# Cosine and sine parts in the two partition halves: three transform stages of a spectral block as pairs of half-array matmuls

## The chip, the cores and the metric

The kernel runs on one core of a Trainium2 chip. The metric is the device time of one execution in microseconds (us), as the median of several runs. TensorE is called PE here, its weight loads PEld; VectorE is DVE, ScalarE ACT, GpSimd POOL, and SyncE SP, whose instructions are almost all DMA issues.

## What is computed

The reference is one block, forward and backward. Its forward half takes x (2048 tokens of 512 channels), normalises the rows and modulates them, filters them in the frequency domain, and sends the sum through a second normalisation and a two-layer network with a squared ReLU. All gradients are returned too.

```python
def _A_ref(x, w_r, w_i):                     # spectral filter
    X = rfft2(x.astype(float32), axes=(-2, -1))      # 2048 x 257, complex
    X = X * (w_r + 1j * w_i)
    return irfft2(X, s=(2048, 512)).astype(bfloat16)
def _B_ref(x, w1, b1, w2, b2):               # 512 -> 1792 -> 512
    h = relu(x @ w1 + b1) ** 2
    return h @ w2 + b2
h = layernorm(x) * (1 + ca) + sa;  x = x + ga * _A_ref(h, w_r, w_i)
h = layernorm(x) * (1 + cb) + sb;  out = x + gb * _B_ref(h, w1, b1, w2, b2)
# returned: out, and the gradients of x, w_r, w_i, w1, b1, w2, b2, c, w_mod
```

The gradient of the filter is a transform of the same kind, so transforms run twice: a forward pass and a backward pass.

## The kernel before

The Fourier transforms are done as matmuls with tables of cosines and sines. A token's number is split as p*16 + t, with p on the 128 partitions and t counting 16 tiles. The forward transform has three stages:

- f1 (`spec_f1_half`, L289, in the forward pass; `spec_f1_row`, L281, in the backward pass): 128-point transform over p. The result goes to UT, with 128 channels on the partitions.
- f2 (L324 to L338): transform over the channels with the table Cd. For each of 8 groups gi and two halves hh, four matmuls (L332) take a 128x128 block of UT as weights and stream 128 columns of Cd; the cosine columns go to the first 256 columns of a PSUM bank, the sine columns to the rest. ACT then copies both banks (L336) to AE with a factor, once per group. One matmul more (L329) adds the constant term in the first group of the forward pass.
- f3 (`f3`, L311 to L323): the 16 tiles are combined with the twiddle table LF. For each gi, hh and each of the two output parts o (real, imaginary), two matmuls of 257 columns (L318) add the cosine and the sine part up in PSUM; this takes LF in three variants, the third being the negated first, which ACT makes (L248, L1175, L1318). ACT copies the result out (L320), and DVE multiplies it with the filter (`cmul`, L411 to L418).

The inverse has g1 (`spec_g1`, L342), g2 (L367, matmuls in L372) and g3 (L378, L382). In g1, for each of 16 n = 2*gi+hh, four matmuls of 128 columns (L352) and two of 256 (L355) take 128x128 blocks of the filtered spectrum Z as weights and stream the table LG, again in three variants (L855, L1354). DVE and ACT copy its PSUM tiles to CS in turn (L360, L362).

The rest of PE's time goes to the two-layer network: L841 (products with the output's gradient, "back products", which fill gaps in the first transform), L1013 and L1042 (the two layers and their gradients), L1287 and L1386 (weight gradients, which fill gaps in the second transform). Column sums (L908, L1238, L1396, L1444) use a quarter of the array's columns each, four at a time, by `tile_position=(0, q)` with q = 0, 32, 64, 96; L459 uses one row strip.

The order of the work is not left to the program text. `ORDER` (L477) lists, for each of PE, ACT, DVE, POOL and SP, the numbers of its instructions as the program emits them, in the order in which they are to run; `set_order` (L574) chains them. Each engine works through its list strictly in that order. Data dependencies are kept with semaphores beside it. The lists hold 2428 matmuls, 470 ACT, 775 DVE and 52 POOL instructions and 290 DMA issues of SP.

Two forms of the code matter for the change, the inner loops of f3 and of g1:

```python
for cs in range(2):                                                              # L317
    nc.tensor.matmul(ps[:, o, 0:DF], lhsT=K["LF"][gi][:, o + cs, hh, :],
                     rhs=ae[:, hh, 256 * cs:256 * cs + DF], start=(cs == 0), stop=(cs == 1))
for ri in range(2):                                                              # L351
    nc.tensor.matmul(ps[:, 0, P * y:P * y + P], lhsT=Z[gi][:, hh, ri, 2 * y:255 + 2 * y:2],
                     rhs=K["LG"][:, n // 4, ri + y, n % 4, :], start=(ri == 0), stop=(ri == 1))
```

Of the kernel before, what the change touches and what calls it, by code (L numbers as in the profile page):

```python
# [9 lines left out]
AF = mybir.ActivationFunctionType  # L10
# [32 lines left out]
def w_parts(rows, gi):  # L43

    v = rows.rearrange("(q h g) f -> q h g f", h=2, g=16)
    if gi > 0:
        return [(0, 64, v[:, :, gi, :]), (64, 64, v[:, ::-1, 16 - gi, :])]
    c = rows.rearrange("(q c g) f -> q c g f", c=4, g=16)
    return [(0, 64, v[:, :, 0, :]), (64, 32, c[:, 0:2, 8, :]), (96, 32, c[:, 3:1:-1, 8, :])]
# [25 lines left out]
def build_basic(tc, constp):  # L75
# [10 lines left out]
    nc.vector.memset(K["ones_q"][:, 0:1], 1.0)  # L86
    pid = constp.tile([P, 1], I32, name="pid")
# [8 lines left out]
def build_ta(tc, K, constp, g, pspool):  # L96
    nc = tc.nc
    kh = g.tile([P, 8, 2, 2, 4], I32, name="kh")
    for r in range(2):
        nc.gpsimd.iota(kh[:, :, :, r, :], pattern=[[1, 8], [16, 2], [32, 4]], base=0, channel_multiplier=0)  # L100
    for h, (base, step) in enumerate(((8, 48), (24, 16))):
        nc.gpsimd.iota(kh[:, 0, h, :, 2:4], pattern=[[0, 2], [step, 2]], base=base, channel_multiplier=0)
    nc.gpsimd.iota(kh[:, 0, 0, 1, 0:1], pattern=[[0, 1]], base=64, channel_multiplier=0)
    off = g.tile([P, 8, 2, 2, 4], I32, name="kh_off")
    nc.gpsimd.memset(off[:, :, :, 0, :], 96)
    nc.gpsimd.memset(off[:, :, :, 1, :], 0)
    nc.gpsimd.memset(off[:, 0, 0, 1, 0:1], 96)
    v = g.tile([P, P], I32, name="ta_v")
    nc.vector.scalar_tensor_tensor(out=v, in0=kh.rearrange("p a h r b -> p (a h r b)"), scalar=K["pidf"],
                                   in1=off.rearrange("p a h r b -> p (a h r b)"), op0=ALU.mult, op1=ALU.add)  # L110
# [13 lines left out]
def build_cd(tc, K, cpool, g):  # L124
# [3 lines left out]
    nc.gpsimd.iota(fr[:, 0:256], pattern=[[2, 2], [2, 128]], base=0, channel_multiplier=0)  # L128
# [13 lines left out]
    nc.vector.tensor_scalar(sn[:, 0:256:255], sn[:, 0:256:255], math.sqrt(0.5), None, op0=ALU.mult)  # L142
# [34 lines left out]
def iotas_lf(tc, g):  # L177
    nc = tc.nc
    sm = g.tile([P, 6, 4], I32, name="lf_sm")
    nc.gpsimd.iota(sm[:, 0, :], pattern=[[1, 4]], base=0, channel_multiplier=0)  # L180
    nc.gpsimd.iota(sm[:, 1, :], pattern=[[-1, 4]], base=3, channel_multiplier=0)
    nc.gpsimd.iota(sm[:, 2, :], pattern=[[0, 2], [1, 2]], base=0, channel_multiplier=0)
    nc.gpsimd.iota(sm[:, 3, 0:2], pattern=[[1, 2]], base=0, channel_multiplier=0)
    nc.gpsimd.iota(sm[:, 3, 2:4], pattern=[[-1, 2]], base=1, channel_multiplier=0)
    nc.gpsimd.iota(sm[:, 4, 0:2], pattern=[[1, 2]], base=2, channel_multiplier=0)
    nc.gpsimd.iota(sm[:, 4, 2:4], pattern=[[-1, 2]], base=3, channel_multiplier=0)
    krs = []
    for q in range(4):
        kr = g.tile([P, 2, 2, 2, 64], I16, name="lf_kr", bufs=4)
        nc.gpsimd.iota(kr[:, :, :, 0, :], pattern=[[1, 2], [16, 2], [32, 64]], base=2 * q, channel_multiplier=0)  # L190
        nc.gpsimd.iota(kr[:, :, :, 1, :], pattern=[[-1, 2], [-16, 2], [32, 64]], base=32 - 2 * q, channel_multiplier=0)
        if q == 0:
            nc.gpsimd.iota(kr[:, 0, :, 1, 0:32], pattern=[[16, 2], [64, 32]], base=8, channel_multiplier=0)
# [5 lines left out]
def build_lf(tc, K, cpool, g, sm, krs):  # L199
    nc = tc.nc  # L200
    V = nc.vector
    ti = g.tile([P, 3], I32, name="lf_ti")
    V.tensor_single_scalar(ti[:, 0:1], K["pid"], 3, op=ALU.logical_shift_right)
    V.tensor_single_scalar(ti[:, 1:2], K["pid"], 4, op=ALU.bitwise_and)
    V.tensor_single_scalar(ti[:, 2:3], K["pid"], 3, op=ALU.bitwise_and)
    tf = g.tile([P, 3], FP32, name="lf_tf")
    V.tensor_copy(tf, ti)
    t, r4, sl = tf[:, 0:1], tf[:, 1:2], tf[:, 2:3]
# [90 lines left out]
def make_ae(nc, pool):  # L299
    AEs = [pool.tile([P, 2, 514], BF16, name=f"AE{i}") for i in range(2)]  # L300
    for ae in AEs:
        nc.gpsimd.memset(ae[:, :, 256:257], 0.0)
# [1259 lines left out]
```

## Time and profile before

| what | value |
|---|---|
| time, median of 3 runs | 407.01 us (406.58 to 407.49) |
| span of the profiled execution, first to last instruction | 402.6 us |
| what lies around the span, by that median | 4.4 us |
| ACT busy | 278.5 us (69%) |
| DVE busy | 342.4 us (85%) |
| HBM traffic over the span | 36.35 MB read, 33.19 MB written |

The profile is of one execution. Busy time counts an instruction from start to end; PE's matmuls overlap (the end of one is modelled), so the distance between the starts of two matmuls tells what one costs, and the busy share does not. A row of the timeline gives the start, the length, the engine, the line, the operation, the tile written and those read, and how many like instructions were merged into it; idle time before it and what ended that stand in brackets. A row of the windows gives busy time and number of instructions for each engine in a stretch, then the granted TensorE clock, the DMA share and GB/s.

### The profile page before, as it was taken

To read this page: it belongs to the slowest core of one execution; us is meant where nothing else is said; L and a number is where in the kernel's file an instruction comes from. 1 tells how busy PE (TensorE), PEld (TensorE's weight loads), DVE (VectorE), ACT (ScalarE), POOL (GpSimd) and SP (SyncE) were. 2 spreads that over 40 slices of the span, in tenths; PEclk is the share of its full clock that TensorE was granted. 3 is DMA by queue.
4 is the path that set the end of the run, shared out by engine and by line. 5 is a ranking of instruction groups with operands and counts; after the bars stand their busy time and mean duration, and the time that the engine had idled before them with its cause. 6 is when DMAs were issued, how large, how long until landed. Compare 5 with 4: busy or idle time off the path is not lost. (4 is left out here: it accounts for less than half of the span.)

```text
span 402.6 us, 6952 instructions
## 1 busy us (share of the span) xinstructions
PE 386.3 (96%) x2428; PEld 201.8 (50%) x2428; DVE 342.4 (85%) x831; ACT 278.5 (69%) x501; POOL 14.0 (3%) x56
## 2 busy tenths in 40 slices
PE   4899999999999999999999999999999999999895
PEld 1354566665444444444444445455655675444344
DVE  5989879969897799989898999947889958897993
ACT  4559899879870596169636857457668456988693
POOL 4520100000000000000000000000000000000000
PEclk9699999999999999999999999999999999999999
DMA  8999999588595689788977889969999899999997
GB/s 255 251 208 271 232 191 270 169 192 276 140 235 140 179 230 147 216 186 210 223 193 163 192 215 239 281 170 281 315 278 283 236 326 180 182 275 234 237 278 257
DMA packets 141643, 90.97 MB, mean 226 GB/s; under 512 B 95778, under 2 KB 127528, under 8 KB 141096
## 3 DMA queue, kind: packets, MB, share of 16 engines
q1 hardware_dynamic: 140900, 89.93, 90.6%
q10 hardware_dynamic: 708, 0.59, 0.5%
q8 instruction: 19, 0.31, 0.3%
q14 instruction: 16, 0.13, 0.1%
HBM read 36.35 MB, written 33.19 MB: 173 GB/s over the span
## 5 line engine op out<-in xcount | busy, mean ns | idle before, releaser
L1287 PEld LDWEIGHTS <-h_sb 128*128 128x128 bf16 x256 | 24.7, 98 | 21.4 <-issue 0.4
L1042 PEld LDWEIGHTS <-gab 128*128 128x128 bf16 x224 | 21.5, 98 | 25.0 <-DVE gab L1020 0.6
L1013 PEld LDWEIGHTS <-w 128*128 128x128 bf16 x224 | 21.3, 98 | 25.0 <-issue 1.8
L841 PEld LDWEIGHTS <-w2T 128*128 128x128 bf16 x224 | 21.3, 98 | 22.5 <-issue 2.9
L1287 PE MATMUL mm_0s<-gab,h_sb 128*128 128x384 bf16 (+1 forms) x160 | 30.2, 342 | 0.0
L1042 PE MATMUL og_0s<-w1T,gab 128*128 128x512 bf16 x112 | 25.9, 379 | 0.1
L1042 PE MATMUL og_1s<-w1T,gab 128*128 128x512 bf16 x112 | 25.8, 379 | 0.0
L336 ACT ACTIVATE AE<-psB 128x1024 bf16<-128x1024 f32 x16 | 22.1, 1383 | 2.8 <-PE psB L332 2.8
L1013 PE MATMUL mm_1s<-h2T,w 128*128 128x512 bf16 x84 | 21.6, 379 | 0.0
L1287 PE MATMUL mm_1s<-gab,h_sb 128*128 128x512 bf16 (+1 forms) x96 | 20.8, 370 | 0.0
L1013 PE MATMUL mm_0s<-h2T,w 128*128 128x512 bf16 x80 | 20.5, 379 | 0.0
L841 PE MATMUL mm_1s<-gT_0s,w2T 128*128 128x512 bf16 x56 | 15.4, 394 | 1.1 <-DMA w2T<-in_B_w_dram 0.9
L841 PE MATMUL mm_0s<-gT_0s,w2T 128*128 128x512 bf16 x56 | 15.3, 397 | 0.8 <-DMA w2T<-in_B_w_dram 0.6
L1013 PE MATMUL pst<-h2T,w 128*128 128x512 bf16 x60 | 15.4, 379 | 0.0
L372 PEld LDWEIGHTS <-utcs 128*128 128x128 bf16 x128 | 10.3, 97 | 8.7 <-issue 2.4
L1386 PE MATMUL mm_0s<-g_sb,hn_1s 128*128 128x512 bf16 x64 | 14.5, 379 | 0.0
L841 PE MATMUL mm_1s<-gT_1s,w2T 128*128 128x512 bf16 x56 | 14.4, 379 | 0.0
L841 PE MATMUL mm_0s<-gT_1s,w2T 128*128 128x512 bf16 x56 | 14.4, 379 | 0.0
L845 ACT CAST gab<-mm_1s 128x512 bf16<-128x512 f32 x20 | 12.4, 620 | 2.2 <-PE mm_1s L841 2.2
L1386 PE MATMUL mm_1s<-g_sb,hn_0s 128*128 128x512 bf16 (+1 forms) x64 | 12.8, 352 | 0.3 <-ACT gw_0s L1387 0.3
L332 PEld LDWEIGHTS <-utcs 128*128 128x128 bf16 x128 | 9.3, 97 | 4.8 <-issue 1.8
L1386 PEld LDWEIGHTS <-hn_0s 128*128 128x128 bf16 x80 | 7.7, 98 | 6.6 <-issue 1.0
(652 smaller groups left out, 1050.2 us busy)
## 6 DMA issues: line engine op xcount, KB each, us to landing
w<-in_B_w_dram SPq DMA_DIRECT2D x2, 1792.0 KB, 8.8
Z<-wz_dram SPq DMA_DIRECT2D x4, 514.0 KB, 4.4
Xb<-xs_dram SPq DMA_DIRECT2D x4, 514.0 KB, 5.9
x_sb<-in_A_x_dram SPq DMA_DIRECT2D x2, 1024.0 KB, 6.3
n_dram<-x_sb SPq DMA_DIRECT2D x4, 512.0 KB, 5.1
h_dram<-h2r SPq DMA_DIRECT2D x8, 256.0 KB, 2.7
h_sb<-h_dram SPq DMA_DIRECT2D x4, 512.0 KB
g_sb<-in_grad_out_dram SPq DMA_DIRECT2D x2, 1024.0 KB
```

Source lines behind the costliest of these rows:

```text
L332: nc.tensor.matmul(ps[:, hh, P * co:P * co + P], lhsT=UT[:, c, 2 * gi + hh, :, :], rhs=K["Cd"][:, P * c:P * c + P], start=not extra, stop= ...
L336: nc.scalar.activation(dst, ps.rearrange("p r (s e f) -> p (r s) e f", s=2, e=2), AF.Copy, scale=EF_S)
L372: nc.tensor.matmul(ps[:, P * i:P * i + P], lhsT=CS[:, t, i].rearrange("p a b -> p (a b)"), rhs=K["Cf"][:, i, :], start=True, stop=True)
L841: nc.tensor.matmul(ps, lhsT=w2T[:, dc, fc * P:(fc + 1) * P], rhs=gT[b][:, :, dc, :], start=(dc == 0), stop=(dc == 3))
L845: nc.scalar.copy(out=gaT[b][:, fc, :], in_=ps)
L1013: nc.tensor.matmul(ps, lhsT=w1[:, dc, (fc + i) * P:(fc + i + 1) * P], rhs=h2T[b][:, :, dc, :], start=(dc == 0), stop=(dc == 3))
L1042: nc.tensor.matmul(ps, lhsT=lhs(fc), rhs=rhs[:, fc, :], start=(fc == 0), stop=(fc == NFC - 1))
L1287: nc.tensor.matmul(blocks(ps, fb), lhsT=h2_sb[:, t, dc * P:(dc + 1) * P], rhs=gh_rows(t, fb), start=(t == 0), stop=(t == NT - 1))
L1386: nc.tensor.matmul(ps[:, 0:w], lhsT=hns[fc][:, t, :], rhs=g_sb[:, t, c:c + w], start=(t == 0), stop=(t == NT - 1))
```

## The change

The cosine part of f2 now goes to the partitions 0 to 63 and the sine part to 64 to 127. UT is laid out in 32 blocks of 64 columns in place of 16 of 128. `tile_position=(0, 64 * cs)` places a matmul in one half of the array's columns, `(64 * b, 0)` in one half of its rows.

- f2: each 128-wide matmul becomes two with 64 weight columns, one for each half of the PSUM partitions: 256 matmuls of 128 columns in both passes together in place of 128.
- f3: the sum over cosine and sine part is now made inside one matmul (its 128 rows hold both), so each (gi, hh, o) has two matmuls of 64 weight columns and 257 streamed columns, one for each half of the output, in place of two full ones. LF has two variants, no negated one.
- g1: each n has 12 matmuls of 64 rows, in pairs on the two row halves: 4 of 128 columns and 8 of 64. The PSUM tile has two banks and three buffers (before: one bank, six buffers). LG has two variants.
- A POOL instruction after each copy to AE moves one column and clears another (the sine column 256). Tables that the transforms need (TA, Cd, LF) are generated in another order of rows, with more and smaller POOL instructions.
- The 12 negating copies of ACT and 4 of DVE are gone. The filter's rows are read and written in smaller pieces.
- `ORDER` is new for all five engines: 2749 matmuls, 458 ACT, 774 DVE and 84 POOL instructions and 310 DMA issues.

```diff
 def f3(gi):
     for o in range(2):
-        for cs in range(2):
-            nc.tensor.matmul(ps[:, o, 0:DF], lhsT=K["LF"][gi][:, o + cs, hh, :], rhs=ae[:, hh, 256 * cs:256 * cs + DF],
-                             start=(cs == 0), stop=(cs == 1))
+        for b in range(2):
+            m = slice(64 * b, 64 * b + 64)
+            nc.tensor.matmul(ps[m, o, 0:DF], lhsT=K["LF"][gi][:, o, hh, m], rhs=ae[:, hh, b, :], start=True, stop=True, tile_position=(0, 64 * b))
...
-            ps = psB_pool.tile([P, 2, 512], FP32, name="psB")
+            ps = psB_pool.tile([P, 2, 2, 256], FP32, name="psB")
...
-                for c in range(4):
-                    co = (0, 3, 1, 2)[c]
-                    nc.tensor.matmul(ps[:, hh, P * co:P * co + P], lhsT=UT[:, c, 2 * gi + hh, :, :], rhs=K["Cd"][:, P * c:P * c + P],
-                                     start=not extra, stop=(c == 3 if extra else True))
+                for b in (1, 0):
...
+                    for e in range(2):
+                        for cs in range(2):
+                            c = 2 * e + cs
+                            nc.tensor.matmul(ps[64 * cs:64 * cs + 64, hh, b, P * e:P * e + P], lhsT=UT[:, c, 2 * (2 * gi + hh) + b, :, :],
+                                             rhs=K["Cd"][:, P * c:P * c + P], start=not extra, stop=(e == 1 if extra else True), tile_position=(0, 64 * cs))
...
+            end = ae.rearrange("p r b f -> p (r b) f")[64:P]
+            nc.gpsimd.tensor_tensor(end[:, :, 256::-256], end[:, :, 0:1].broadcast_to([64, 4, 2]), K["one0"][64:P, None, :].broadcast_to([64, 4, 2]), op=ALU.mult)
...
 def spec_g1(tc, K, Z, CS, after=None):
-    with Slots(tc, name="psG", bufs=6, space=PSUM) as psG_pool:
+    with Slots(tc, name="psG", bufs=3, space=PSUM) as psG_pool:
...
+                def part(b, o, y, w, f0):
+                    m = slice(64 * b, 64 * b + 64)
                     for ri in range(2):
+                        yield (ps[:, b, hh, o, 64 * y:64 * y + w], Z[gi][m, hh, ri, f0:f0 + 255:2], K["LG"][m, n // 4, ri, n % 4, 64 * y:64 * y + w],
+                               ri == 0, ri == 1, (64 * b, 0))
+                for args in ((1, 0, P, 1), (0, 0, 64, 0), (0, 1, 64, 2)):
+                    for pair in zip(part(0, *args), part(1, *args)):
+                        for o, l, r, first, last, pos in pair:
+                            nc.tensor.matmul(o, lhsT=l, rhs=r, start=first, stop=last, tile_position=pos)
...
-        nc.scalar.activation(LF[:, q, 2], LF[:, q, 0], AF.Copy, scale=-1.0)
...
-        nc.vector.tensor_scalar(K["LG"][:, q, 2], K["LG"][:, q, 0], -1.0, None, op0=ALU.mult)
...
-    UT = utcs.tile([P, 4, 16, NT, 8], BF16, name="utcs")
+    UT = utcs.tile([P, 4, 32, NT, 4], BF16, name="utcs")
...
-    CS = utcs.tile([P, NT, 4, 16, 8], BF16, name="utcs")
+    CS = utcs.tile([P, 4, NT, 16, 8], BF16, name="utcs")
```

More of the change, by code (lines that the diff above doesn't have):

```diff
@@ L829 @@
     for q in range(4):
[L830 removed]
+        nc.sync.dma_start(LF_dram[q], K["LFall"][:, q])
     psM.release()
@@ L1210 @@
     gmp = Slots(tc, name="gmp", bufs=1, side="right")
-    LF2 = [lf2.tile([P, 3, 4, P], BF16, name=f"LFb{4 + 2 * g}") for g in range(2)]
+    LF2 = [lf2.tile([P, 2, 4, P], BF16, name=f"LFb{4 + 2 * g}") for g in range(2)]
     K["LF"] += [LF2[g // 2][:, :, 2 * (g % 2):2 * (g % 2) + 2] for g in range(4)]
@@ L1400 @@
         load_hn()
-    CS = utcs.tile([P, NT, 4, 16, 8], BF16, name="utcs")
+    CS = utcs.tile([P, 4, NT, 16, 8], BF16, name="utcs")
     def scale_g(gi):
```

189 lines of the change are left out of this document (98 added, 91 removed), and 156 rows, old and new, of the table ORDER.

## The prediction

> **What bounds the kernel now.** I read the page first, then the windows of the stages that the change touches, then PE's waits, then the timeline row by row for the distance between matmuls. From the page:
>
> ```profile
> span 402.6 us, 6952 instructions
> ...
> PE 386.3 (96%) x2428; PEld 201.8 (50%) x2428; DVE 342.4 (85%) x831; ACT 278.5 (69%) x501; POOL 14.0 (3%) x56
> ...
> PE   4899999999999999999999999999999999999895
> ```
>
> PE is busy from end to end; but its records overlap, so this alone proves little. The windows show the four stages that change: first f2 and f3 (50 to 74), first g1 (74 to 84), second f2 and f3 (263 to 314), second g1 (314 to 328).
>
> ```profile
> 50.00:74.00 24.00, 23.55 (x191) 15.30 (x191) 20.64 (x55) 24.00 (x37) 0.00 (x0) 1.00 0.99 205
> 74.00:84.00 10.00, 10.00 (x110) 7.96 (x109) 9.03 (x18) 7.80 (x15) 0.00 (x0) 1.00 0.80 230
> 263.00:314.00 51.00, 50.80 (x383) 29.42 (x376) 40.08 (x91) 34.77 (x56) 0.00 (x0) 1.00 0.91 265
> 314.00:328.00 14.00, 14.00 (x135) 10.32 (x134) 12.34 (x26) 7.36 (x16) 0.00 (x0) 1.00 0.97 283
> ```
>
> The columns are PE, PEld, DVE, ACT, POOL, clock. The clock is 1.00 throughout. In the first stretch ACT is busy 24.00 of 24.00 us as well, and DVE 20.64; in the others PE stands alone. PE's waits are few. The longest, and the one that a changed stage has:
>
> ```profile
> PE sm_ps L718 <- POOL ident masks.py:199: 4.0, 1, 4.0
> ...
> PE psB L332 <- ACT AE L336: 0.2, 1, 0.2
> ```
>
> So what PE need not stream comes off the end, unless ACT or DVE then ends last. What a matmul costs is the distance of starts:
>
> ```profile
> 59.12 0.61 PE L332 MATMUL psB<-Cd,utcs 128*128 128x128 bf16 x8
> 59.56 0.61 PE L318 MATMUL psC_1s<-AE,LF 128*128 128x257 bf16 x4
> 60.03 0.38 PE L318 MATMUL psC_0s<-AE,LF 128*128 128x257 bf16 x2
> 60.25 1.02 PE L841 MATMUL mm_1s<-gT_0s,w2T 128*128 128x512 bf16 x4
> ...
> 62.16 1.02 PE L841 MATMUL mm_0s<-gT_0s,w2T 128*128 128x512 bf16 x4
> 63.02 0.39 PE L318 MATMUL psC_1s<-AE,LF 128*128 128x257 bf16 x2
> ...
> 80.40 0.28 PE L352 MATMUL psG_1s<-LG,Z 128*128 128x128 bf16 x2
> 80.51 0.38 PE L355 MATMUL psG_1s<-LG,Z 128*128 128x256 bf16 x2
> 80.73 0.38 PE L355 MATMUL psG_2s<-LG,Z 128*128 128x256 bf16 x2
> ```
>
> Eight f2 matmuls take 59.56 - 59.12 = 0.44 us, 55 ns each; two f3 matmuls 60.25 - 60.03 = 0.22, 110 ns; four back products 63.02 - 62.16 = 0.86, 215 ns; in g1 128 columns 0.11 / 2 = 55 ns and 256 columns 0.22 / 2 = 110 ns. Each has its weight load, and hides it. The counts, from the groups by line (each load has one matmul):
>
> ```profile
> L332 PEld LDWEIGHTS <-utcs 128*128 128x128 bf16 x128 | 9.3, 97 | 4.8 <-issue 1.8 <-ACT utcs L286 0.4
> ...
> L352 PEld LDWEIGHTS <-Z 128*128 128x128 bf16 x128 | 9.1, 98 | 1.4 <-issue 0.2
> ...
> L318 PEld LDWEIGHTS <-LF 128*128 128x128 bf16 x64 | 5.8, 97 | 2.3 <-issue 0.3
> ...
> L318 PEld LDWEIGHTS <-LFb 128*128 128x128 bf16 x64 | 5.4, 97 | 1.7 <-issue 0.5
> ...
> L355 PEld LDWEIGHTS <-Z 128*128 128x128 bf16 x64 | 5.3, 98 | 0.4
> ```
>
> Now f2 is 128 x 55 ns = 7.0 us, f3 128 x 110 ns = 14.1 us, g1 128 x 55 + 64 x 110 ns = 14.1 us, both passes together.
>
> **The change, part by part.** Whether two half-array matmuls run side by side is the first question. The column sums already use quarters of the array's columns:
>
> ```profile
> 151.57 1.02 PE L1013 MATMUL pst<-h2T,w 128*128 128x512 bf16 x4
> 152.52 0.39 PE L908 MATMUL acc<-gp_0s,ones_q 128*32 128x512 bf16 x1
> ...
> 152.53 0.39 PE L908 MATMUL acc<-q_0s,ones_q 128*32 128x512 bf16 x1
> 152.75 0.38 PE L908 MATMUL acc<-gp_0s,ones_q 128*32 128x512 bf16 x1
> ...
> 153.19 0.38 PE L908 MATMUL acc<-q_1s,ones_q 128*32 128x512 bf16 x1
> 153.50 0.61 PE L1013 MATMUL mm_1s<-h2T,w 128*128 128x512 bf16 x2
> ```
>
> Four start within 0.01 us, the next four 0.23 us after the first: four 512-column matmuls in the time of one. Column parts do run side by side.
>
> *f3*: 128 full matmuls become 64 pairs, at 110 ns a pair 7.0 us: a gain of **7.0**.
>
> *f2*: 128 full matmuls become 128 pairs of the same width. Side by side they cost the same, and they cannot cost less, since each half streams 128 columns; one behind the other they cost 7.0 more. Taken: **0**, by the quarters.
>
> *g1*: each of 32 blocks (16 n, two passes) now has two pairs of 128 columns (55 ns each) and four of 64. For the short ones the bounds are half of 55, 28 ns, and this row:
>
> ```profile
> 10.13 0.54 PE L752 MATMUL sm_ps<-sacol,wm_2s 128*128 128x1 bf16 x16 [1.43 <-DVE sacol L722]
> 10.53 1.60 PE L737 MATMUL mod_ps<-wm_0s,gab 128*128 128x512 bf16 x4
> ```
>
> 16 matmuls of one column, each with its own load, take 0.40 us: 25 ns is the least distance seen, and two such make a pair 50 ns at most. So g1 costs 32 x (2 x 55 + 4 x 28 to 50) ns = 7.1 to 9.9 us, a gain of 4.2 to 7.0. I take 35 ns, nearer to the low end because the quarters start within 0.01 us of each other: 8.0 us, a gain of **6.1**. On small matmuls "TensorEngine Tiling (Array Packing)" of the Trainium skill, section Instruction Overhead, says that about 60 cycles go by for each however short it is, and that one should not split a dimension that is already small; the row of 25 ns agrees, and since 64 columns lie above that floor, the rule would give the low end of 28 ns and 0.9 us more gain.
>
> *Mode switches*, which speak against the change. Before the quarters above, four L1013 matmuls take 152.52 - 151.57 = 0.95 us in place of 0.86: 0.09 lost on entering. The last quarter starts 0.31 us before the next full matmul in place of 0.215: 0.10 on leaving. The first four quarters last 0.23 in place of 0.215, and the first full matmul after them is a little late too. I take 0.105 us a switch. Sorting both PE lists of `ORDER` by stage, the list before goes 30 times from full to part of the array, back, or from one part form to another, the new one 94 times: first f2/f3 25 (13 blocks, with back products between), first g1 12, the rest in the second pass and at the sums. 64 more cost 64 x 0.105 = 6.7 us: a loss of **6.7**. The price was seen at quarters and may differ at halves: from below it is 0, and from above nothing near shows more.
>
> *ACT in the first pass.* ACT is full there, and PE gets no faster than ACT lets it:
>
> ```profile
> 52.44 1.19 ACT L235 ACTIVATE lf_w_1s<-lf_v,npi 128x1024 bf16<-128x1024 int16 x1
> ...
> 59.83 1.39 ACT L336 ACTIVATE AE<-psB 128x1024 bf16<-128x1024 f32 x1
> 61.01 0.64 ACT L320 CAST Xs_1s<-psC_1s 128x514 bf16<-128x514 f32 x1
> 61.48 0.66 ACT L845 CAST gab<-mm_1s 128x512 bf16<-128x512 f32 x1
> 61.95 0.68 ACT L320 CAST Xs_1s<-psC_0s 128x514 bf16<-128x514 f32 x1
> ```
>
> By distance of starts a copy to AE costs 1.18 us, a copy of f3 or of a back product 0.47. The stage keeps 8 and 16 of the former two, and the new ACT list puts 6 back-product copies and one table step (L235, 1.19 us) between: 8 x 1.18 + 16 x 0.47 + 6 x 0.47 + 1.2 = 21.0 us. The negating copies that stood there are gone. PE has in the stage 64 x 55 ns (f2) + 32 x 110 ns (f3) + 52 back products x 215 ns (52 in both lists) + 25 switches = 3.5 + 3.5 + 11.2 + 2.6 = 20.8 us, before 3.5 + 7.0 + 11.2 = 21.7 of the 24. Two engines at 21 us, chained through one AE buffer pair and one PSUM tile, do not both run without gaps: I charge **1.0** (bounds 0 and 2.5, at which the stage stays as it is).
>
> *DVE in the second pass.* It is busy 40.08 of 51 us and 12.34 of 14; the two stages lose some 3 us of PE time there. What is late next is DVE, by products for g1: charged **0.5**, bounds 0 and 2.
>
> *POOL's new instruction* lies between the copy to AE and f3. A table step, and the only POOL arithmetic in the trace:
>
> ```profile
> 4.50 0.23 POOL L102 IOTA kh<- 128x4 int32 x2
> ...
> 10.26 0.22 POOL L402 TENSOR_SCALAR inv<-l_mv_0s 128x2 f32<-128x2 f32 x1 [5.02 <-DVE l_mv_0s L769]
> 10.56 0.72 POOL L403 TENSOR_TENSOR inv<-inv,nhalf 128x2 f32<-128x2 f32 x1
> ```
>
> 0.22 to 0.72 us for 8 elements a row. The wait stands in PE's list before f3; behind it are the back products of that gap. The next group's f2 (0.44 us) starts on the same release and hides 0.44. At the high end 7 gaps of the first pass lose 0.3 each, 2.1 us; in the second pass the weight-gradient matmuls of each gap cover it. It is one multiplication, so I take the low row: **0**.
>
> *The start.* POOL has 16 table steps more, and some five of them stand before table TA, for which DVE already waits:
>
> ```profile
> 4.76 0.35 DVE L109 SCALAR_TENSOR_TENSOR ta_v<-kh,pidf,kh_off 128x128 int32<-128x128 int32 x1 [2.22 <-POOL kh L102]
> ```
>
> At 0.12 us each that is up to 0.6; the others fit into the 5.02 us in which POOL waits. Taken **0.2**. *DMA*: 20 issues more on SP for the same bytes (8 for filter pieces, 12 for their gradients), none of which PE waits for; no charge. *PSUM of g1*: three tiles of two banks in place of six of one; the copies of a block pair now take longer than its matmuls, and the 15 back products and some 58 weight-gradient matmuls that the new list puts into the two g1 stages cover that; without them it would be 1 to 2 us a pass. The 12 ACT and 4 DVE copies that go are counted above where they stood on a full engine.
>
> Sum: -7.0 + 0 - 6.1 + 6.7 + 1.0 + 0.5 + 0.2 = **-4.7 us**. The span of 402.6 would become 397.9. The median before is 407.01, 4.4 above the span, and I carry the difference over: 402.3 us.
>
> **Rivals.**
> 1. *Row halves take turns.* No row shows two row strips at once, so g1's pairs may run one behind the other: 32 x (4 x 55 + 8 x 28) ns = 14.2 us, no gain. Then -4.7 + 6.1 = +1.4: 408.4, **slower**. It decides from the point where g1 keeps less than 1.4 of its 6.1. Against it: column quarters do overlap.
> 2. *Loads of column halves stand in the open.* f2's place: 256 loads for 128 pairs, each pair with 55 ns to hide two. A load is recorded with 97 ns; if both stood in the open f2 would lose 128 x (194 - 55) ns = 17.8 us; it decides from 55 + 4.7 / 128 = 92 ns a pair, above which the kernel is slower. As middle I take 110 ns, the two halves in turn: +7.0, so +2.3, 409.3. Against it: full loads hide behind 55 ns now. In the Trainium skill, "TensorEngine Tiling (Array Packing)", section Restrictions, rules out Fast Weight Load under column tiling, and "TensorE: Matmul & The Clock Gate", section LDWEIGHTS, gives columns / 1.2 ns, 53 ns for 64 columns; as an estimate from that a pair in turn takes 107 ns, a total of about +1.9. No run here shows such a load against so short a matmul.
> 3. *POOL's step is exposed* (the 0.72 row): -4.7 + 2.1 = -2.6, 404.4.
> 4. *Halves switch cheaper than quarters*, say at half the price: -4.7 - 3.4 = -8.1, 398.9. Nothing in the trace speaks for it but that it is another form.
> 5. *The change does not do what it says*: the new lists do not keep PE filled, and the gain stays as waits: 407.0.
>
> **How the numbers follow.** The forecast (402.3; 399.7 with every term at its low end, 405.7 with g1 and ACT at their high ends and the rest as taken) gets 0.60, rival 1 0.08, rival 2 0.08, rival 3 0.10, rival 4 0.08, rival 5 0.06. About 0.2% or 0.8 us is what a measurement of this kernel can tell from no change. Faster by more than that: the forecast, rivals 3 and 4, together 0.78. Same: rival 5, with some of the edges, 0.07. Slower: rivals 1 and 2 less a part that ends at zero, 0.15. The range takes in rivals 3 and 4 and ends at rival 5: 398.2 to 407.2; outside lie the slower cases and a small tail below.
>
> **What would show it.** Right: f3 pairs start within 0.01 us, the next pair 0.11 later; f2 pairs 55 to 60 ns apart; short g1 pairs 28 to 50 ns; about 0.1 us lost at each change between full and half array; the first f2/f3 stage about 21 to 22 us. Wrong: f2 pairs over 92 ns, or g1 halves one after the other; PE waiting on POOL before f3; waits of PE on ACT or DVE of more than 2 us in the changed stages.

## The result: slower by one per cent, and the profile after

| | before | after |
|---|---|---|
| time, median of 17 runs each, taken in turn | 406.96 us (404.69 to 408.70) | 411.66 us (407.23 to 413.78) |
| ratio, 95% interval | | 1.0102 [1.0082, 1.0122] |
| profiled execution: span | 402.6 us | 410.0 us (time 411.87) |

Ratios are of fast executions alone: one slow one of the changed kernel (413.78 us) and two of e12 below (653 and 785 us) are not in them.

The kernel became 4.2 us slower by the ratio, where 4.7 us of gain were predicted: the sign was wrong, and the time lies above the range. The two profiled spans differ by 7.4 us, more than the medians. The runs of before beside the experiments have 1.7 to 1.9 us around their spans, so by estimate its profiled execution took about 404.4 us, at the quick end of the 17 above; some 2.5 of the 7.4 us are spread between executions. The 4.4 us that the prediction carried from span to median were for the most part that spread; its difference of 4.7 does not hang on them.

The first part of the page after:

```profile
span 410.0 us, 7674 instructions
...
PE 381.7 (93%) x2749; PEld 189.1 (46%) x2749; DVE 340.3 (83%) x830; ACT 276.0 (67%) x490; POOL 23.4 (6%) x88
...
PE   5499899769999999999999999999999999999993
...
PEclk9999999989999999999999999999999999999998
```

PE has 4.6 us less busy time (its records overlap, so this is a hint and no measure), in a span that is 7.4 us longer. The holes are in the first ten slices, 100 us: 54 at the start where there was 48, and a 7 with a 6 around 80 us, where the clock dips too. PE's waits name them:

```profile
PE mm_1s L856 <- DVE gT_0s L775: 5.7, 1, 5.7
PE psG_0s L375 <- issue: 4.4, 1, 4.4
PE sm_ps L733 <- DMA vrow<-in_c_dram: 3.1, 1, 3.1
PE psC_0s L328 <- POOL AE L351: 1.2, 1, 1.2
```

Before, PE's longest wait was 4.0 us, at the very start, and the next 1.4. Now the first back product (L856) waits 5.7 us for DVE, the first g1 product (L375) 4.4 us, and the first small matmul for c 3.1 us. POOL's new step cost 1.2 us, once.

The windows of the changed stages, cut at their first and last matmuls (columns: length, then PE, PEld, DVE, ACT, POOL busy, clock, DMA share, GB/s). Before:

```profile
50.01:73.67 23.66, 23.21 (x190) 15.11 (x190) 20.30 (x55) 23.66 (x37) 0.00 (x0) 1.00 1.00 208
74.80:83.48 8.68, 8.68 (x104) 7.38 (x103) 7.72 (x15) 6.51 (x12) 0.00 (x0) 1.00 0.90 254
```

After, with the gap between the two in the middle row and the second pass's f2 and f3 behind:

```profile
57.57:81.20 23.63, 21.68 (x246) 10.82 (x246) 19.11 (x47) 21.65 (x31) 3.75 (x8) 1.00 1.02 176
81.20:85.89 4.69, 0.27 (x6) 0.03 (x2) 4.08 (x9) 3.52 (x6) 0.00 (x0) 0.97 1.31 179
85.89:96.20 10.31, 10.09 (x206) 6.43 (x207) 6.20 (x10) 5.05 (x9) 0.00 (x0) 0.85 1.09 325
273.77:317.73 43.96, 43.96 (x426) 23.60 (x425) 34.61 (x81) 31.15 (x48) 3.25 (x8) 1.00 0.90 258
```

The first f2/f3 stage begins 7.6 us later than before and is no shorter; 4.7 us pass before g1; g1 runs at 0.85 of the clock. The second pass's f2 and f3 have no wait: 43.96 of 43.96 us busy. The balance, by the starts of the same matmuls in the timelines of before and after (e11 is an experiment below; its program is the same, in another order):

| stretch | before | after | e11 |
|---|---|---|---|
| start to first f1 | 16.82 | 23.78 | 19.12 |
| first f1 to first f2 | 33.19 | 33.79 | 34.48 |
| first f2 to first layer-1 product | 55.18 | 60.00 | 54.76 |
| to the second pass's first f2 | 158.20 | 156.20 | 157.09 |
| from there to the last matmul | 134.46 | 129.22 | 129.23 |
| last matmul to the end | 4.79 | 7.04 | 5.61 |

Back products are spread alike in all three (8, 84 and 132 in the first three stretches); the last stretch has 8 column sums more after and 3 products less. So the second pass gained 5.2 us, and the first lost 12.4 before layer 1 began. These are single executions: in the other profiles that leave the second pass's PE list as it is, its stretch to the last matmul takes 127.54 to 130.82 us, and in e6 (the kernel before, with one load moved) 135.59.

### The profile page after: what moved, and what is told of

It reads as the page before. It is cut to its first block, busy times and chain, and to the rows that moved or that the text cites. A ratio compares the mean times of both kernels' runs of the same rounds, so it can differ in the third digit from the quotient of the medians.

```text
span 410.0 us, 7674 instructions
## 1 busy us (share of the span) xinstructions
PE 381.7 (93%) x2749; PEld 189.1 (46%) x2749; DVE 340.3 (83%) x830; ACT 276.0 (67%) x490; POOL 23.4 (6%) x88
## 3 DMA queue, kind: packets, MB, share of 16 engines
HBM read 36.35 MB, written 33.19 MB: 170 GB/s over the span
## 4 chain that ended last, share of the span: by engine, by line
PE 71%; ACT 9%; DVE 8%; DMA 7%; issue 1%; POOL 1%; ACTq 0%; SPq 0%; DVEq 0%
PE og_0s L1057 12%; PE og_1s L1057 12%; PE mm_0s L1301 7%; PE mm_1s L1301 5%; PE mm_1s L1027 4%; PE mm_0s L1027 4%; PE mm_1s L856 3%; PE pst L1027 3%; PE mm_0s L856 3%; DMA gT_1s<-in_grad_out_dram 2%; DMA vrow<-in_c_dram 2%; PE mm_0s L1400 2%; PE psB L345 2%; ACT gab L860 1%; PE mm_1s L1400 1%
## 5 line engine op out<-in xcount | busy, mean ns | idle before, releaser
L856 PEld LDWEIGHTS <-w2T 128*128 128x128 bf16 x224 | 20.9, 100 | 31.7 <-issue 12.8
L1301 PEld LDWEIGHTS <-h_sb 128*128 128x128 bf16 x256 | 23.4, 98 | 22.3 <-issue 3.0
L1301 PE MATMUL mm_0s<-gab,h_sb 128*128 128x384 bf16 (+1 forms) x160 | 31.8, 343 | 0.0
L856 PE MATMUL mm_1s<-gT_0s,w2T 128*128 128x512 bf16 x56 | 17.5, 415 | 5.7 <-DVE gT_0s L775 5.7
L856 PE MATMUL mm_0s<-gT_0s,w2T 128*128 128x512 bf16 x56 | 16.1, 399 | 0.7 <-DVE gab L858 0.7
L856 PE MATMUL mm_1s<-gT_1s,w2T 128*128 128x512 bf16 x56 | 14.7, 379 | 0.8 <-ACT gab L860 0.8
L856 PE MATMUL mm_0s<-gT_1s,w2T 128*128 128x512 bf16 x56 | 14.7, 379 | 0.0
L1070 ACT CAST G_0s<-og_0s 128x512 bf16<-128x512 f32 x4 | 2.3, 586 | 16.1 <-PE og_0s L1057 16.1
L391 PEld LDWEIGHTS <-utcs 128*128 128x128 bf16 x128 | 9.6, 98 | 7.7 <-issue 1.7
L375 PEld LDWEIGHTS <-Z 64*128 64x128 bf16 x384 | 8.9, 99 | 8.8 <-issue 8.2
```

The lines of the kernel that those rows point to most:

```text
L375: nc.tensor.matmul(o, lhsT=l, rhs=r, start=first, stop=last, tile_position=pos)
L391: nc.tensor.matmul(ps[:, P * i:P * i + P], lhsT=CS[:, i, t].rearrange("p a b -> p (a b)"), rhs=K["Cf"][:, i, :], start=True, stop=True)
L856: nc.tensor.matmul(ps, lhsT=w2T[:, dc, fc * P:(fc + 1) * P], rhs=gT[b][:, :, dc, :], start=(dc == 0), stop=(dc == 3))
L1070: nc.scalar.copy(out=st["G"][:, j % 2, :], in_=P_.pop(j))
L1301: nc.tensor.matmul(blocks(ps, fb), lhsT=h2_sb[:, t, dc * P:(dc + 1) * P], rhs=gh_rows(t, fb), start=(t == 0), stop=(t == NT - 1))
```

## The experiments

All edits but that of e8 only move numbers within the lists of `ORDER`: each number is an instruction of that engine, counted as the program emits it. Ratios are to the kernel before, run beside each. Rows are of one execution, which need not be a typical one of its kernel.

**e1: c first.** ACT issues the load of c (number 0, L690) and of `w_mod` (1, L698). Before, c went first. The change's list has them the other way round:

```profile
0.73 0.47 ACTq L698 DMA_DIRECT2D wm_2s<-in_w_mod_dram  x1
1.23 0.65 ACTq L690 DMA_DIRECT2D vrow<-in_c_dram  x1
...
9.23 0.17 ACT L734 ACTIVATE sigcol<-sm_ps 128x4 f32<-128x4 bf16 x1 [2.85 <-PE sm_ps L733]
```

In the same rows of before c's sigmoid runs at 4.22:

```profile
0.73 0.55 ACTq L675 DMA_DIRECT2D vrow<-in_c_dram  x1
...
4.22 0.17 ACT L719 ACTIVATE sigcol<-sm_ps 128x4 f32<-128x4 bf16 x1 [0.64 <-PE sm_ps L718]
```

```diff
-ACT  1 0 2 9 8
+ACT  0 1 2 9 8
```

> Only the first two entries of the ACT list are exchanged: the 1 KB load of c is issued ahead of the 512 KB load of w_mod. Theory A (the changed kernel loses its time at the start because c lands late, and everything that hangs on c is late by that): c lands some 3 us earlier, the cast ccolf moves from 9.44 us to about 6.6, the first back product from 18.71 to about 16, the first f2 from 57.57 to about 55, and the time falls by 2.5 to 3 us against the changed kernel's 411.7, to about 409. Theory B (the start is bound by the DVE list, or by the second half of x and the w2 transposes): ccolf moves, but the first f2 stays within 0.7 us of 57.57 and the time at 411 to 412.

1.0037 [1.0009, 1.0064], 405.95 us. The copy of c (L735) comes at 6.60 in place of 9.44, the first back product at 17.67 (18.71), the first f2 at 56.09 (57.57). Two numbers changed places and more than half of the loss was gone. The remaining start did not follow: the 5.7 us wait for gT_0s stayed, and a new one of 2.1 us for `wm_2s` came. The rows explain the time only in part: the first f2 moved by 1.5 us where 2.5 were expected, and the profiled execution is the quickest of the twelve (402.94 us).

**e6: the same exchange in the kernel before.** This asks whether the order of two loads costs that much by itself, without any half-array matmul.

```diff
-ACT  0-3 5 4
+ACT  1 0 2-3 5 4
```

> The kernel before with one thing changed: on ACT the 512 KB load of w_mod is issued ahead of the 1 KB load of c, as the changed kernel has it. Theory A: c lands some 4 us later, ccolf moves from 5.83 us to about 9, gb2x and the four scalings are late by about 2 to 3 us, the first f2 by 1.5 to 3 us, the time is 1.5 to 3 us longer (1.004 to 1.007). Theory B (the start hangs on the landing of w2 and on row statistics, which do not need c in this kernel): first f2 late by under 0.7 us, time within 0.002.

1.0064 [1.0042, 1.0087], 407.66 us. Its sigmoid:

```profile
9.20 0.17 ACT L719 ACTIVATE sigcol<-sm_ps 128x4 f32<-128x4 bf16 x1 [5.63 <-PE sm_ps L718]
```

The first f2 comes 3.13 us later, just above the 1.5 to 3 expected, and PE waits 9.0 us for c. The kernel before becomes slower by 0.6% (2.6 us) through one load behind another, so this part of the loss is shown on both kernels.

**e2: gT_0s scaled first.** DVE's list goes through the row statistics (L783, 0.66 us each) before the scaling of gT_0s (30 to 33, L775), on which the first back product waits.

```diff
-DVE  104 27 34 25 ... 48 30 54 56 31-32 49 57 39 33 41
+DVE  104 30-33 27 34 25 ... 48 54 56 49 57 39 41
```

> Only the DVE list is changed: the four scalings of the first transposed gradient tile stand directly behind the cast of b1, ahead of the row statistics. If theory A holds, the PE wait of 5.7 us in front of the first back product goes (it starts at about 13.2 us, when w2 lands), but the wait comes back in front of the first f1, which still waits for the late rows: first f1 at 23.8 to 25, first f2 between 56.5 and 58.5, time 410.5 to 412.5. If the position of the scalings is what costs (theory B), the first f2 moves forward by about 5 us and the time falls to 406 to 407.

1.0107 [1.0071, 1.0143], 409.83 us: nothing gained. The first back product starts at 12.97 as it did before (13.04), but the wait moved behind it:

```profile
PE psA_1s L303 <- DVE fold_u_0s L267: 5.4, 1, 5.4
```

The first f1 starts at 23.40, after at 23.78. DVE does the same work up to f1's input in either order; as long as its chain starts with c at some 9 us, the 5.7 us wait is only the place at which its lateness meets PE. The row statistics, which need no c, stand behind the steps on c in the change's list, so DVE is idle until c comes (first row, after); before, it ran them from 6.13 on (second row):

```profile
9.44 0.16 DVE L735 CAST ccolf<-sm_ps 128x4 f32<-128x4 bf16 x1 [4.03 <-ACT sigcol L734]
```

```profile
6.13 0.69 DVE L768 BATCH_NORM_STATS2 l_st_3s<-x_sb 128x6 f32<-128x512 bf16 x1
```

e5 below, which brings c early and the statistics ahead of its steps, has the first f1 at 18.85; with c alone (e1) it is at 22.50.

**e3: LG early.** SP makes the table LG with four transposes out of LF (L869). In before they were issued at 49.82 to 63.69; after and in e3:

```profile
63.40 1.33 SPq L869 DMA_TRANSPOSE LG<-LF  x1
64.82 5.38 SPq L708 DMA_TRANSPOSE gT_1s<-in_grad_out_dram  x1
...
76.28 7.13 SPq L869 DMA_TRANSPOSE LG<-LF  x3
```

```profile
69.63 4.87 SPq L869 DMA_TRANSPOSE LG<-LF  x3
```

```diff
-SP  45 13 37 97 40 86 90 38 83 46 50 42 47 44
+SP  45 13 50 42 47 37 97 40 86 90 38 83 46 44
```

(45, 50, 42, 47 are LG; 13 is gT_1s; 37, 40, 38 store LF; 97, 86, 90, 83 copy filter pieces, L1040; 46 stores LG.)

> Only the SP list is changed: the last three transposes of the g1 tables (LG) stand directly behind the transpose of gT_1s, ahead of seven DRAM copies and table stores. Theory C (g1 starts 4.7 us behind the last f3 because the LG transposes are issued late): the gap falls to about 1.2 us as in the kernel before, and the time by about 3.4 us, to about 408.3. Rival D (the gap is the spectrum products on DVE, the PSUM copies or the clearing on POOL): the gap stays over 3.5 us and the time at 411 to 412.

1.0068 [1.0042, 1.0093], 407.69 us. The gap between f3 and g1 is 0.96 in place of 4.69 us, so it lay in SP's list, where four filter copies and four stores of tables stood ahead of LG; the first layer-1 product comes 3.6 us earlier. The time fell by less: 0.34%, 1.4 us, and its interval overlaps the change's a little.

**e4: all at once.** c first on ACT; on DVE three row statistics and the scaling of gT_0s earlier; on SP the second half of x loaded ahead of a load of w_mod (7 and 10 exchanged), LG early, and nine filter copies (L1040) moved behind LG:

```diff
-SP  17 95 20 124 36 119 32 93 88 33-34 29 126 84 91 117 39 45 13 37 97 40 86 90 38 83 46 50 42 47 44
+SP  17 20 36 32-34 29 39 45 13 50 42 47 95 124 119 93 88 126 84 91 117 37 97 40 86 90 38 83 46 44
```

> Lists alone again, all three together: c first on ACT, the second half of x ahead of the second half of w_mod on SP, three row statistics and the four scalings earlier on DVE, the LG transposes early and nine DRAM copies behind them on SP. If the half-array stages gain what the prediction priced (about 4.7 us against the kernel before) and only loads and lists lost it, first f2 comes at 51 to 53 us, g1 starts about 1.2 us behind the last f3, and the time is 402 to 404, below the kernel before (407). If the half-array stages themselves cost more than priced, the time stays at 406 or above although the waits are gone.

1.018 [1.0141, 1.0219], 411.52 us: a miss, slower than the change itself. The gap before g1 is 0.95 us as it should be, but the filter copies now stand ahead of the stores of Xs (f3's result, L887). ACT in g2 waits for the last of them, which was issued at 88.86 (columns of the windows as above):

```profile
97.96 0.60 ACT L393 ACTIVATE Tsb_0s<-psT 128x512 bf16<-128x512 f32 x1 [7.24 <-DMA xs_dram<-Xs_3s]
```

```profile
90.00:94.00 4.00, 1.28 (x9) 0.44 (x7) 0.69 (x1) 0.72 (x2) 0.00 (x0) 0.91 1.11 369
94.00:98.00 4.00, 0.00 (x0) 0.10 (x1) 0.00 (x0) 0.04 (x1) 0.00 (x0) 0.50 1.14 158
98.00:102.00 4.00, 3.39 (x15) 1.74 (x15) 0.00 (x0) 2.70 (x6) 0.00 (x0) 0.50 0.85 220
```

PE does nothing from 94 to 98, and works at half clock for the 4 us behind. SP's list is one chain: here, what was moved out of the way of one wait lay in the way of the next.

**e5: start and LG, without the filter copies.** e1, e3, and DVE:

```diff
-DVE  22 12 122 17 23-24 104 27 34 25 35-36 26 28 37 44 29 53 38 45-46 40 47 55 48 30 54 56 31-32 49 57 39 33 41
+DVE  22 27 34 12 25 122 17 23 35-36 26 28 37 44 53 24 104 30-33 29 38 45-46 40 47 55 48 54 56 49 57 39 41
```

(27, 34, 25 are row statistics, which need no c; 12 to 24 are the steps on c, 104 is b1.)

> Lists alone, without the moved DRAM copies of the run before: c first on ACT, the first eight row statistics as soon as x is there and the four scalings right behind gb2x on DVE, the three late LG transposes directly behind that of gT_1s on SP. If the half-array stages gain what was priced and only lists and loads lost it: first back product at about 13.0 us, first f1 at 17 to 19.5, first f2 at 51 to 53.5 (57.57 in the changed kernel, 50.01 before), g1 at most 1.4 us behind the last f3, time 0.985 to 0.994 of the kernel before. Rival: the half-array stages or their new copies and clearings cost more than priced; then the anchors move as said and the time still stays at 0.998 of the kernel before or above.

1.0026 [1.0000, 1.0053], 406.38 us. The start holds: the first back product at 12.98, the first f1 at 18.85, f2 at 53.32. But a new wait stands before g1. DVE stands still at the scaling of gT_1s, whose transposing load (SP's 13) has not landed yet, and behind it in DVE's list is the cast that PE waits for:

```profile
70.33 0.88 DVE L775 TENSOR_SCALAR gT_1s<-gT_1s,gb2x 128x512 bf16<-128x512 bf16 x3 [2.50 <-DMA gT_1s<-in_grad_out_dram]
```

```profile
76.36 1.15 PE L856 MATMUL mm_0s<-gT_0s,w2T 128*128 128x512 bf16 x4 [2.55 <-DVE gab L858]
```

Of its two waits the second comes from the first: DVE, which works its list strictly in order, hands on the late DMA to PE, which waits for the cast behind it.

**e9: that scaling later.** e5, and DVE's 222 220 219 221 (scaling of gT_1s) from behind 181 to ahead of 183.

> The lists of the run with the start and LG mended, and one move more on DVE: the four scalings of the fourth gradient tile (gT_1s, whose transpose lands at 70.3 us and which PE first reads at 94.6) stand behind the spectrum products, in place of in the middle of them. Theory H (DVE waits 2.5 us in order for that transpose, the copy of the back products behind it is late, PE waits 2.5 us for the copy and then runs at half the clock from 77.5 to 82.5 us): the PE wait at 74 us goes, the clock in 76 to 84 us stays at 1.00, g1 ends some 4 to 5 us earlier (90.62 to about 86), and the time falls from 1.003 of the kernel before to 0.991 to 0.994. Rival (a wait costs itself alone): the PE wait goes, the time falls by 2.5 us at most, to 0.996 or 0.997. Rival (the copies on DVE and ACT bound this stage): the wait comes back elsewhere in 70 to 92 us and the time falls by under 1 us.

1.0070 [1.0037, 1.0104], 409.75 us: a miss. The wait at 74 us is gone and f3 ends 2.2 us earlier than in e5, g1 2.1 us earlier. Then the wait of e4 returns, since g2 now comes before Xs has landed:

```profile
PE psY L401 <- ACT Tsb_0s L393: 3.6, 1, 3.6
```

```profile
90.00:94.00 4.00, 0.48 (x3) 0.10 (x1) 0.69 (x1) 0.53 (x1) 0.00 (x0) 0.82 1.21 210
94.00:98.00 4.00, 3.88 (x16) 1.92 (x16) 0.45 (x2) 2.70 (x6) 0.00 (x0) 0.50 0.80 248
```

The first layer-1 product is at 115.56, 3.6 us later than in e5 (111.98).

**e10: the last loads earlier.** e9, and SP's loads of `wmc` (287, 288, L471) ahead of 279. After, a DVE step at 398.89 waits 3.23 us for one of them.

> The run beside this one, and one move more on SP: the last two loads of w_mod (wmc) are issued ahead of the last transposes of h, the second of them some 9 us earlier (at about 379 in place of 388 us). Theory I (it lands late, DVE waits 3.2 us for it, the stores behind it on SP pile up): the DVE wait for wmc_1s goes and the stretch from the last matmul to the end of the span falls from 7.0 us to about 5, the time by 1.5 to 2 us more than in the run beside it. Rival (the stores at the end are bound by SP's own issue rate): the DVE wait goes, the stretch stays over 6.5 us and the time the same.

1.0071 [1.0038, 1.0103], 408.85 us. In the profile the time from the last matmul to the end is 5.85 in place of e9's 7.24 us; the ratio is the same. The tail's share in the time is not shown.

**e11: Xs stored first.** e10, and SP's stores of Xs (44 41 49 52) directly behind LG, the filter copies behind the next loads:

```diff
-SP  50 42 47 37 97 40 86 90 38 83 46 44 51 41 43 49 48 52 64 56 54 69 61 55 67
+SP  50 42 47 44 41 49 52 37 40 38 46 51 43 48 64 56 54 69 61 55 67 97 86 90 83
```

> The lists of the run with the tail load mended, and one move more on SP: the four stores of the spectrum (xs) are issued directly behind the LG transposes, the stores of LF and LG behind them, and the last four DRAM copies (wz) behind the transposes of w1. Theory J (the first copy of g2's result, Tsb, waits 3.7 us because the last spectrum store lands 9.1 us after its issue, queued behind eleven transfers that nobody needs before 262 us; and PE then runs at half the clock): the PE wait for Tsb goes, the clock from 88 to 100 us stays at 1.00, the first layer-1 product comes at 109 to 111.5 us in place of 115.5, and the time falls from 1.007 of the kernel before to 0.990 to 0.996, below it. Rival (w1's transposes or x's loads, now behind, take the wait over): the wait appears between 90 and 115 us in front of another tile and the time stays above 1.002.

0.9943 [0.9915, 0.9971], 402.57 us beside 405.22: faster than both kernels, with the program of the change and nothing else than its order altered. Its span is 400.3 us. Rows of the page, and the windows of e9's wait:

```profile
PE   5788999799999999999999999999999999999984
...
PEclk9999999999999999999999999999999999999999
```

```profile
90.00:94.00 4.00, 3.70 (x27) 1.93 (x25) 2.38 (x6) 3.41 (x8) 0.00 (x0) 1.00 1.04 212
94.00:98.00 4.00, 4.00 (x26) 1.99 (x24) 3.93 (x12) 3.95 (x10) 0.00 (x0) 1.00 1.27 185
```

The hole at 90 us is closed, the clock is 1.00, and layer 1 begins at 108.36, 7.2 us earlier than in e9. Not all of this comes of the wait of 3.6 us that went and the half clock behind it: g1's last matmul is already 1.6 us earlier (87.00 for 88.56). Both executions have a gap of 1.1 us on PE that ends at 78.8 (e9) and 78.9 (e11); behind it e9 ran at half the clock and e11 did not:

```profile
79.00:82.00 3.00, 3.00 (x8) 1.03 (x7) 3.00 (x8) 0.84 (x2) 0.00 (x0) 0.50 1.07 162
```

```profile
79.00:82.00 3.00, 3.00 (x24) 1.28 (x23) 3.00 (x9) 1.65 (x4) 0.00 (x0) 1.00 1.02 391
```

The edit is not seen to cause this: e12, with the same SP list, ran at half the clock there too, and the mean clock of the profiled execution of e11 (0.998) is the highest of its twelve. So some of the 7.2 us is luck of this execution; the verdict is from all twelve. e11 is 1.6% below the change by the two ratios (1.0102 and 0.9943).

**e12: more statistics before the steps on c.** e11, and DVE:

```diff
-DVE  44 53 24 104 30-33 29 38 45-46 40 47 55 48 54 56 49 57
+DVE  44 53 45-47 55 54 56 24 104 30-33 29 38 40 48-49 57
```

> The lists of the run with the spectrum stores first, and one move more on DVE: all eight row statistics of the first half of x stand ahead of gb2x and of the four scalings (two of them stood behind). Theory K (what the start has still lost, first f1 at 19.12 us in place of 16.82 before, hangs on the last two statistics, POOL's reciprocal roots of them and the scaling of these rows): the first f1 moves to 17 to 18 us, the first back product at most 0.7 us later than 13.16, the first f2 from 53.60 to 52 to 52.8, and the time falls by 0.8 to 1.6 us, to 0.990 to 0.993 of the kernel before. Rival (PE, whose eight back products and two rows of modulation then stand in front of f1, is the bound there): the first f1 stays over 18.6 us and the time at 0.994.

0.9935 [0.9911, 0.9959], 403.01 us beside 405.18. The first back product comes at 14.64, later than e11's 13.16, the first f1 at 18.82 (19.12): the same time as e11 within the intervals. Moving the remaining statistics ahead gains nothing more. What PE waits for there is `wm_2s` (2.3 us) and gb2x (2.9 us); what bounds the remaining 2 us stays open.

**e7: more mode switches.** One PE list of the second pass woven more finely: groups of four f2 matmuls between full ones, 58 changes more, the same matmuls.

```diff
-PE  1713-1724 1729-1732 1725-1728 1813-1816
+PE  1713-1716 1813 1717-1720 1814 1721-1724 1729-1732 1815 1725-1728 1816
...
```

> The changed kernel with the PE list of the second pass woven finer: in seven places a block of half-array matmuls and the full-array products behind it are dealt out four by four, which makes some 58 more changes between half and full array; the same matmuls otherwise. Price of the prediction, 0.105 us per change: the stage from the first f2 to the last f3 of the second pass grows from 43.96 us to about 50, the time by about 6 us to 1.025 of the kernel before. Rival (a change costs half as much or less): stage 47 or below, time at most 1.018. Rival (no price at all, only PE waits): stage within 0.7 us of 43.96 unless the waits view shows it.

1.0298 [1.0263, 1.0333], 417.90 us. The timeline of e7 in that stage:

```profile
288.65 0.30 PE L345 MATMUL psB<-Cdb,utcs 128*64 128x128 bf16 x4
288.88 0.66 PE L1301 MATMUL mm_0s<-gab,h_sb 128*128 128x384 bf16 x3
289.47 0.30 PE L345 MATMUL psB<-Cdb,utcs 128*64 128x128 bf16 x4
289.71 0.50 PE L1301 MATMUL mm_0s<-gab,h_sb 128*128 128x384 bf16 x2
290.14 0.30 PE L345 MATMUL psB<-Cdb,utcs 128*64 128x128 bf16 x4
```

Four f2 matmuls, two pairs, should take 0.11 us and take 288.88 - 288.65 = 0.23; two products of 384 columns, 0.162 each by the distance inside a group, take 290.14 - 289.71 = 0.43 in place of 0.32. That is about 0.1 us each way, as predicted from the quarters; 58 times 0.095 is 5.5 us. The stage grew from 43.96 to 57.43 us, 13.5: PE's waits there add 2.8 us (1.6 for the copy to AE, three others of 1.2 together), and a clock of 0.89 and 0.69 at 316 to 324 us, half rate for some 3.4 us, at most 1.7. Some 3.5 us of the 13.5 are not explained. So the rows show the price of one change, and the time of e7 is no measure of it.

**e8: PE kept busy at the start.** In the profile after, the first back products lie twice as far apart as they should:

```profile
18.71 0.59 PE L856 MATMUL mm_1s<-gT_0s,w2T 128*128 128x512 bf16 x1 [5.68 <-DVE gT_0s L775]
19.09 1.06 PE L856 MATMUL mm_0s<-gT_0s,w2T 128*128 128x512 bf16 x2
19.94 1.49 PE L856 MATMUL mm_1s<-gT_0s,w2T 128*128 128x512 bf16 x3
```

0.85 / 2 = 0.42 us each, while the clock's row says 1.00. e8 adds 24 products of ones, whose result nothing uses, and PE's list puts them ahead of the back products:

```diff
-    for k in range(10):
+    for k in range(34):
```

> The changed kernel with 24 more of its ten idle products of ones (they feed nothing), placed on PE in the wait of 5.7 us ahead of the first back product, some 5.2 us of them. Theory F (a PE that has stood idle for some us runs at half speed for the next 3 to 4 us): the eight first back products follow at 0.22 us each in place of 0.42, the first f1 comes 0.9 to 1.5 us earlier, and the time falls by about 1 to 1.5 us. Rival G (first f1 waits for the folds on DVE anyway): the products run at 0.22 us, the first f1 stays within 0.4 us of 23.78 and the time at 1.010 of the kernel before.

```profile
18.53 0.38 PE L856 MATMUL mm_1s<-gT_0s,w2T 128*128 128x512 bf16 x1
18.75 0.59 PE L856 MATMUL mm_0s<-gT_0s,w2T 128*128 128x512 bf16 x2
```

0.22 us each: with PE kept busy ahead of them, the back products run at full speed. The first f1 comes at 21.64, 2.1 us earlier, but in this execution c also came 0.7 us sooner (first small matmul at 8.35 for 9.01), so some of this may be c's. In the time it is 1.0086 [1.0054, 1.0118], 408.97 us: 0.16% better than the change, inside the intervals, so inconclusive there; the profiled execution (405.70 us) is the quickest of its seven.

## Why the prediction was wrong

**The step that failed** is the one on the new order: "20 issues more on SP for the same bytes (...), none of which PE waits for; no charge", together with the start at 0.2 us. The prediction sorted the lists of PE and ACT by stage and counted what they hold; it never set the issues of DMAs in ACT's and SP's lists, or DVE's list, against the moment at which the data is used. Three places in these lists cost the change its gain: c's load behind a larger one (e1: 0.65%; e6: 0.64% on the kernel before), the row statistics behind the steps on c in DVE's list (first f1 at 22.50 in e1, 18.85 in e5; no run prices this alone), and LG's transposes behind filter copies and stores (e3: 0.34%). Behind them stood two more that show only once these are mended: gT_1s (e5) and Xs (e4, e9). With all of them mended the same matmuls are 0.6% faster than before (e11, and e12 again), and with none 1.0% slower. That it is order and not arithmetic is thereby shown: e11 changes lists only. What stood in the sum at nothing and 0.2 us is worth 1.6% between these two orders, some 6.5 us. Half of the forecast gain came, 2.3 of 4.7 us. No run gives the kernel before's lists the same care, so how much of the 0.6% the half-array matmuls alone are worth is not shown.

**The mechanism was in rival 5**, "the new lists do not keep PE filled", and its size was wrong: it lost the gain and no more, 407.0, with a chance of 0.06. A wait can cost more than the gain it eats, for two reasons that the runs show: it has a length of its own, unrelated to the gain (5.7, 4.4, 3.1 us), and the clock can go to half behind it.

**The terms of the sum held.** From the second pass after:

```profile
281.83 0.64 PE L345 MATMUL psB<-Cdb,utcs 128*64 128x128 bf16 x16
282.30 0.39 PE L328 MATMUL psC_1s<-AE,LFb 128*64 128x257 bf16 x4
282.52 0.39 PE L328 MATMUL psC_0s<-AE,LFb 128*64 128x257 bf16 x4
282.84 0.39 PE L1301 MATMUL mm_0s<-gab,h_sb 128*128 128x512 bf16 x1
...
321.49 0.41 PE L375 MATMUL psG_0s<-LGb,Z 64*128 64x128 bf16 x12
...
321.96 0.39 PE L375 MATMUL psG_1s<-LGb,Z 64*128 64x128 bf16 x12
```

- f3: two pairs in 282.52 - 282.30 = 0.22 us, 110 ns a pair. As predicted, 7.0 us.
- f2: eight pairs in 0.47 us, 59 ns each. Predicted 55; 128 x 4 ns = 0.5 us more at most. Rival 2 is out: its turning point was 92 ns. The estimate of 107 ns that it worked out from the Trainium skill, "TensorE: Matmul & The Clock Gate", section LDWEIGHTS, does not hold in this trace.
- g1: a block of 12 in (321.96 - 321.49) / 2 = 0.235 us. Predicted 0.25; gain 14.1 - 32 x 0.235 = 6.6 in place of 6.1. Rival 1 (0.444 us a block) is out.
- Switches: the last pair before a full matmul takes 282.84 - 282.52 = 0.32 in place of 0.22 us, so 0.10. Rival 4 is out, by this and by e7.
- POOL: 1.2 us once, in the first pass. Taken 0, bound 2.1. This was a named sign of being wrong, and it did show, at this small price.
- ACT in the first pass: predicted 21 to 22 us for the stage, 23.63 after, 22.39 in e11, where PE's and DVE's waits are less.

The second pass comes nearest to what the arithmetic is worth by itself, as PE's waits in it are short (the longest 1.0 us before, 0.8 after): from its first f2 to the last matmul 134.46 became 129.22 us, -5.2. The prediction's terms for it were -3.5 for f3, -3.05 for g1, 27 of the 64 switches at +2.8 and DVE at +0.5, together -3.2. g1 was better by 0.25 and DVE's 0.5 was not seen; matmuls moved across the border make another 0.2. About 1 us of gain is left over, which is within the spread of single executions (127.54 to 130.82 us, above). For the first pass the terms gave -1.5 with the start; it came out at +12.4 after and +3.2 in e11. Against its terms e11 lost 2.1 us at the start, 1.3 in f1 (whose matmuls the change leaves as they are), 1.3 from f2 to layer 1 and 0.8 behind the last matmul; it won 2.0 in the second pass and 1.1 in the layers between. So -4.7 became -2.35 in its profile. In f1 PE waits some 2.9 us for DVE's folds and the copies of back products, where before it waits 1.1 for loads; why these come late, and what holds up the start, is not settled.

**The signs that were named** looked in the wrong place. Those for a right forecast came true for the pairs of f2, f3 and g1 and for the price of a change, though not for the first f2/f3 stage (23.63 us), and the forecast was wrong all the same. That for a wrong one, "waits of PE on ACT or DVE of more than 2 us in the changed stages", did not appear there: the long waits lay ahead of f1, and between f3 and g1.

## What to carry to other kernels

Where a change brings a new written-out order, put every list beside the old one, the issues of DMAs first: for each transfer, what is now ahead of it in its queue, and when its data is used. Price an exposed wait by its own length plus a slow clock that may follow it, not by the gain it could eat; and where one list is mended, look for the next late transfer behind it before believing the sum.

## What the runs showed of the hardware

- Where the small load of c is issued 0.5 us behind a larger one by the same engine, it is used later than where it goes first: 5 us in the kernel before (sigmoid at 9.20 in e6 against 4.22), 2.8 us in the changed one (copy of c at 9.44 against 6.60 in e1).
- The clock behind a wait. After (PE, PEld, DVE, ACT, POOL, clock), around the start of g1:

```profile
86.00:87.00 1.00, 1.00 (x31) 1.00 (x30) 0.46 (x1) 0.00 (x0) 0.00 (x0) 0.50 1.07 436
...
89.00:90.00 1.00, 1.00 (x6) 0.50 (x5) 0.00 (x0) 0.59 (x1) 0.00 (x0) 0.98 1.12 398
```

  PE's gap of 4.4 us is followed by some 3.4 us at 0.50. The Trainium skill, "TensorE: Matmul & The Clock Gate", section Part 1: The HAM clock gate, has half rate after about 3.4 us of idle PE, until it has been busy as long. The length at half agrees in these rows; the idle time does not agree in all: the gap of 1.1 us at 78 us was followed by half rate in e9 and not in e11 (rows at e11), one of 2.5 us was in e5 (a mean of 0.50 over 78 to 82 us), and one of 2.6 us was not in e1 (1.00 over 82 to 86 us). What exactly sets it off is open.
- At the start of the changed kernel the matmuls lay 0.42 us apart while the clock's row said 1.00: there the distance of starts tells more than the row. The kernel before starts slowly too (a clock of 0.50 over 11 to 17 us), so the slow clock at the start is not the change's own.
- Pairs on row halves run side by side as those on column halves do, with loads of 64 columns hidden behind matmuls of 55 to 59 ns.
- A store issued at 88.86, behind the filter copies, kept ACT's next step of g2 waiting until 97.96, 9 us later (e4); in e11, with the stores ahead of those copies, no engine waits for it.
